# Block products for two more tiles of batch 0, and a new order of the work beside them

## The chip, the cores and the metric

The kernel runs on one core of a Trainium2 chip. The metric is the device time of one execution in microseconds (us). Before the change it is 262.92 us, the median of 3 runs (262.75 to 263.28).

## The reference, cut to what matters

Attention over blocks (4 batches, 8 heads, 768 rows, head size 64) is followed by a residual layer of 512 channels, in which one product mixes the 768 rows ("tokens") and two products the channels (512 to 2048 to 512). Keys and values are mixed block by block with an 8x8 matrix P, the result of five rounds of normalisation.

```
k_sorted = einsum('bhij,bhjcd->bhicd', P, k_b);  v_sorted likewise
scores = scale * q_b @ k_sb.T;  attn = softmax(scores);  x = attn @ v_sb
a1  = alpha1 * x + beta1
u   = x + lam * einsum('ts,bsd->btd', w_tok, a1)
a2  = alpha2 * u + beta2
out = u + lam * (relu(a2 @ w_ch1) @ w_ch2)
```

## The kernel before, in words

**Stages.** Every instruction of TensorE (PE), VectorE (DVE), ScalarE (ACT), GpSimd (POOL) and of the queue of SyncE (SP) is kept in the order in which the program issues it: the class Engine at line 55 records each one, which is why the profile gives one line, L65, for all, and groups are told apart by their tiles. The last loop of the program (lines 1055 to 1072) goes over 4 batches b and two halves hf of 384 rows each. A half has 16 units "h" (h_unit, line 763: four 128x384 matmuls from a2T and W1p into a buffer h_ps, and a ReLU on ACT into the halves hTa and hTb), and then the second channel product, phase "c".

**The second channel product.** In batch 0 it is done tile by tile (ch_unit, line 766): a tile of 128 rows takes 16 matmuls of 128x512, hT against W2p, and one VectorE addition. From batch 1 on it is done for two tiles at once (ch_pair, line 831): seven products of eight 128x256 matmuls instead of two times sixteen 128x512, named px, py, pz, px, pz, px, py after the buffers that they fill. They use sums and differences of the two tiles (block_sums, line 814: four VectorE operations for each part of the eight slices) and of the quarters of W2p (block_weights, line 798: eight operations of 128x1024 into TWa and TWb, once). Eight VectorE additions add_out take the products out, and some of the products must wait until an earlier addition has read their buffer. The pair numbers 0, 1 and 2 stand for tiles (1,2), (3,4) and (0,5).

**What is put beside it.** The attention of the next batch and the token product stand between the units. They are entered in a table by put(b, hf, kind, n, ...) (line 965): after unit n of phase "h", or after step n of phase "c", run() (line 968) issues the list of that slot. The slots are written out by hand in lines 974 to 1041. What matters here:

- mix_v and mix_k (lines 547, 562) make the mixed values and keys: a few matmuls into mix_ps or kmix_ps, and on ACT one cast for mix_v, four for mix_k into kT. bounce_v and back_v write the values to memory and read them back in another layout, on SP.
- score (line 419) fills sc_ps, and ACT takes the exponential. pv (line 479) multiplies by the values into x_ps; VectorE makes a reciprocal (rcb) and a product (x). After two of them, tails copies three blocks and first_affine does two operations (a): this is what flush and flush_one issue (line 509).
- moe_tok (line 715) is the token product, 6 matmuls of 128x512 into tok_ps, then u on VectorE and a 16-bit copy on ACT; moe_cross turns that copy round with three transposing DMAs on SP (uT), and moe_affine makes a2T of it for the next half.
- scale_weights (line 786) multiplies W2p by lam in four VectorE operations of 128x2048.

**Buffers.** PSUM has two pools: psA with 2 buffers (scores, x_ps, mix_ps, kmix_ps) and psB with 4 (h_ps, tok_ps, ch_ps, px, py, pz). An instruction that takes a buffer waits until its last reader is done.

Of the kernel before, what the change touches and what calls it, by code (L numbers as in the profile page):

```python
# [16 lines left out]
def kernel(  # L17
# [22 lines left out]
    B, H, S, D = q.shape  # L40
# [34 lines left out]
    act = Engine(nc.scalar)  # L75
# [11 lines left out]
    def psa(shape, dtype, name):  # L87
        return pools["psA"].tile(shape, dtype, name=name, tag="psA")
# [458 lines left out]
    def mix_v(b, n, eng):  # L547
        if n == 0:
            mixed[b] = att.tile([128, HB, D], F16, name="mixed", tag="qn" if b == B - 1 else "sums", bufs=1 if b == B - 1 else 2)
        ps = psa([128, 2, 512], FT, "mix_ps")  # L550
        raw = raw_of[(b, 1)][:].rearrange("p t d -> p (t d)")
        for m in range(2):
            pe.matmul(
                ps[:, m, :], bigM[b][:].rearrange("p a x -> p (a x)"),
                raw[:, n * 1024 + m * 512:n * 1024 + (m + 1) * 512], start=True, stop=True,
            )
        eng(
            mixed[b][:, n * 16:(n + 1) * 16, :].rearrange("p t d -> p (t d)"),
            ps[:].rearrange("p m f -> p (m f)"),
        )  # L560

    def mix_k(b, n, engs):
        if n == 0:
            kT_of[b] = att.tile([128, H4, NB, BLK], F16, name="kT", tag="kT", bufs=1)
        ps = psa([128, 8, 128], FT, "kmix_ps")
        raw = raw_of[(b, 0)]
        for tp in range(8):
            pe.matmul(
                ps[:, tp, :], raw[:, 16 * n + 2 * tp:16 * n + 2 * tp + 2, :].rearrange("p t d -> p (t d)"),
                bigP[b][:].rearrange("p a t g i -> p (a t g i)"), start=True, stop=True,  # L570
            )
        dst = kT_of[b][:].rearrange("p g i (th tp par) -> p th (g i) tp par", th=2, par=2)
        for par in range(2):
            for h2 in range(2):
                engs[2 * par + h2](
                    dst[h2 * 64:h2 * 64 + 64, :, :, 8 * n:8 * n + 8, par],
                    ps[par * 64:par * 64 + 64, :, h2 * 64:h2 * 64 + 64].rearrange(
                        "p n (th c) -> p th c n", th=2
                    ),
                )  # L580

    def bounce_v(b):
        for th in range(2):
            sp.dma_start(
                vscr[b, :, th * HB:(th + 1) * HB, :], mixed[b][th * 64:(th + 1) * 64, :, :],
            )
# [128 lines left out]
    def moe_tok(b, kt, ps):  # L715
        u32 = u_of[b]
        tok_part(b, kt, 0, C, ps)
        if b not in u16_of:
            u16_of[b] = moep.tile([128, NT, C], F16, name="u16", tag="u16", bufs=1)
        dve.scalar_tensor_tensor(  # L720
            u32[kt], tok_of[(b, kt)][:], 1.0 / GAIN, x_of[b][:, kt, :], op0=ALU.mult, op1=ALU.add,
        )
        act.copy(u16_of[b][:, kt, :], u32[kt])

    def moe_cross(b, hf):
        uT = uT_of[(b, hf)] = att.tile([128, CT, 384], F16, name="uT", tag="uT", bufs=2)
        for m in range(3):
            sp.dma_start_transpose(
                uT[:, :, m * 128:(m + 1) * 128], u16_of[b][:, 3 * hf + m, :],
            )  # L730

    def moe_affine(b, hf):
        for ci in range(CT):
            affine(b, hf, ci, uT_of[(b, hf)][:, ci, :], act if b and hf else dve)
# [3 lines left out]
    HK = HT // 2  # L738
# [24 lines left out]
    def h_unit(b, hf, m):  # L763
        h_part(b, hf, m, range(CT))
# [200 lines left out]
    def put(b, hf, kind, n, *todo):  # L965
        at.setdefault((b, hf, kind, n), []).extend(todo)
# [18 lines left out]
    pairs = [("s", 0), ("s", 2), ("p", 0), ("s", 4), ("p", 2), ("s", 6), ("p", 4), ("p", 6)]  # L985
    for b in range(1, B):
        p = b - 1
        if b == 1:
            for n in range(3):
                put(0, 0, "h", 11 + n, lambda n=n: mix_v(1, n, act.copy))  # L990
                put(0, 0, "c", 3 + 3 * n, lambda n=n: mix_k(1, n, (act.copy,) * 4))
            put(0, 0, "h", 13, lambda: bounce_v(1))
            put(0, 0, "c", 1, lambda: back_v(1))
            for g in range(H4):
                put(0, 0, "c", (4, 7, 10, 10)[g], lambda g=g: q_turn_late(1, g, (dve.tensor_copy, act.copy)[g % 2]))
            put(0, 0, "c", 11, lambda: loads(2))
            seq = [("s", 0), ("s", 1), ("s", 2), ("p", 0), ("s", 3), ("p", 1), ("p", 2), ("s", 4), ("p", 3), ("s", 5),
                   ("p", 4), ("s", 6), ("p", 5), ("s", 7), ("p", 6), ("p", 7)]
            for at_, (kind, n) in enumerate(seq):
                put(0, 1, "h", at_, (lambda n=n: score(1, n // 2, n % 2, psa)) if kind == "s" else (lambda n=n: pv(1, n // 2, n % 2)))  # L1000
        else:
            for n in range(3):
                put(p - 1, 1, "c", 1 + n, lambda b=b, n=n: mix_v(b, n, act.copy))
                put(p - 1, 1, "c", ((3, 6, 8), (4, 7, 10))[b - 2][n], lambda b=b, n=n: mix_k(b, n, (act.copy,) * 4))
            put(p - 1, 1, "c", 3, lambda b=b: bounce_v(b))
            put(p - 1, 1, "c", 7, lambda b=b: back_v(b))
            for kt in range(NT):
                put(*((0, 1, "h", 13) if b == 2 else (1, 0, "c", 1)), lambda b=b, kt=kt: q_cross(b, kt))
            if b + 1 < B:
                put(p, 0, "h", 3, lambda b=b: loads(b + 1))  # L1010
            for (kind, n), at_ in zip(
                pairs, ((0, "h", 0), (0, "h", 3), (0, "h", 5), (0, "h", 8), (0, "h", 11), (0, "c", 0), (0, "c", 2), (1, "h", 1)),
            ):
                for i in range(2):
                    f = (lambda b=b, n=n + i: score(b, n // 2, n % 2, psa)) if kind == "s" else (lambda b=b, n=n + i: pv(b, n // 2, n % 2))
                    put(p, *at_, f)
            for at_ in ((0, "h", 6), (0, "h", 7), (0, "h", 12), (0, "h", 13), (0, "c", 4), (0, "c", 5), (1, "h", 2), (1, "h", 3)):
                put(p, *at_, flush_one)
        if b == 1:
            put(p, 1, "h", 15, flush)  # L1020
        put(p, 1, "h", 3, lambda b=b: moe_start(b))
        for kt in range(3):
            put(p, 1, *(("c", 4) if b == 1 else ("h", 7 + 2 * kt)), lambda b=b, kt=kt: moe_tok(b, kt, psb))
        put(p, 1, *(("c", 4) if b == 1 else ("h", 11)), lambda b=b: moe_cross(b, 0))
        put(p, 1, "c", 8 if b == 1 else 6, lambda b=b: moe_affine(b, 0))
        for kt in range(3):
            put(b, 0, "h", 2 * kt, lambda b=b, kt=kt: moe_tok(b, 3 + kt, psb))
        put(b, 0, "h", 4, lambda b=b: moe_cross(b, 1))
        put(b, 0, "c", 2, lambda b=b: moe_affine(b, 1))

    for g, m in enumerate((12, 12, 13, 13)):
        put(0, 0, "h", m, lambda g=g: scale_weights(g))
    for n, at_ in enumerate(((0, 1, "c", 7),) * 4 + ((0, 1, "c", 9),) * 4):
        put(*at_, lambda n=n: block_weights(n))
    for b in range(1, B):
        for hf in range(2):
            for at_, lo, hi in ((8, 0, 4), (14, 4, 7), (15, 7, 8)):
                at.setdefault((b, hf, "h", at_), []).insert(0, lambda b=b, hf=hf, lo=lo, hi=hi: block_sums(b, hf, lo, hi))
        put(b, 1, "h", 11, lambda b=b: block_sums(b, 2, 0, 4))
        for at_, lo, hi in ((0, 4, 7), (5, 7, 8)):  # L1040
            put(b, 1, "c", at_, lambda b=b, lo=lo, hi=hi: block_sums(b, 2, lo, hi))

    for m in range(3):
# [10 lines left out]
    for b in range(B):  # L1054
        for hf in range(2):
            for i in range(HT):
                if b or hf or i > 2:
                    h_unit(b, hf, i // 2 + HK * (i % 2) if b else i)
                    run(b, hf, "h", i)
            slot = iter(range(14))  # L1060

            def step(b=b, hf=hf, slot=slot):
                run(b, hf, "c", next(slot))

            if b:
                for n in ((0,), (1, 2))[hf]:
                    ch_pair(b, n, step)
                continue
            for kk in range(3):
                for part in range(4):  # L1070
                    ch_unit(b, hf, kk, (4 * part, 4 * part + 4))
                    step()


# [28 lines left out]
```

## Time and profile before

| | us |
|---|---|
| median of 3 runs | 262.92 |
| the profiled execution | 262.59 |
| its span, from the first to the last instruction | 260.8 |
| TensorE busy, of the span | 248.4 |
| VectorE busy | 175.0 |
| ScalarE busy | 154.6 |
| granted TensorE clock, as a share of full speed | 0.997 |

The 1.8 us between the span and the time of that execution lie around the program. Matmuls are pipelined, so that the busy time of TensorE is not its work at full rate: of eight matmuls in a row the distance from start to start is what counts. In the timeline the bracket behind an instruction tells how long its engine was idle before it and what ended that. A wait in the list of waits is put down to what came last.

By stage, from the timeline of TensorE: 0 to 56 us the start and the first half of batch 0's units; 56 to 70 its second product; 70 to 86.5 the units of the second half, with batch 1's scores; 86.5 to 104 its second product, with the token product of batch 1; then batch 1 (104 to 160), batch 2 (160 to 213) and batch 3 (213 to 261).

### The profile page before, as it was taken

To read this page: it belongs to the slowest core of one execution; us is meant where nothing else is said; L and a number is where in the kernel's file an instruction comes from. 1 tells how busy PE (TensorE), PEld (TensorE's weight loads), DVE (VectorE), ACT (ScalarE), POOL (GpSimd) and SP (SyncE) were. 2 spreads that over 40 slices of the span, in tenths; PEclk is the share of its full clock that TensorE was granted. 3 is DMA by queue.
4 is the path that set the end of the run, shared out by engine and by line. 5 is a ranking of instruction groups with operands and counts; after the bars stand their busy time and mean duration, and the time that the engine had idled before them with its cause. 6 is when DMAs were issued, how large, how long until landed. Compare 5 with 4: busy or idle time off the path is not lost.

```text
span 260.8 us, 5951 instructions
## 1 busy us (share of the span) xinstructions
PE 248.4 (95%) x2371; PEld 159.8 (61%) x2371; DVE 175.0 (67%) x467; ACT 154.6 (59%) x282; POOL 44.3 (17%) x67
## 2 busy tenths in 40 slices
PE   8998899999999999999899999999899899999994
PEld 2566665555655544456665797568656775686783
DVE  6695889486438845759975964299966763462863
ACT  3567767565987588497464686888255004847400
POOL 8759303600091000074000000000000000000000
PEclk9999999999999999999999999999999999999998
DMA  6999999998999967979974169610202132111022
GB/s 101 211 204 187 208 206 215 203 139 186 172 176 176 121 143 171 152 132 182 136 118 119 20 146 169 133 23 0 80 18 45 42 96 69 23 40 40 3 80 80
DMA packets 67535, 31.07 MB, mean 119 GB/s; under 512 B 56674, under 2 KB 63218, under 8 KB 67508
## 3 DMA queue, kind: packets, MB, share of 16 engines
q0 software_dynamic: 26352, 15.34, 45.2%
q1 hardware_dynamic: 41060, 15.33, 33.8%
q8 instruction: 18, 0.29, 0.5%
q14 instruction: 9, 0.07, 0.1%
q10 hardware_dynamic: 96, 0.03, 0.1%
HBM read 32.79 MB, written 8.65 MB: 159 GB/s over the span
## 4 chain that ended last, share of the span: by engine, by line
PE 54%; DVE 19%; issue 2%; SPq 1%; DMA 1%; ACT 0%; DVEq 0%; ACTq 0%
PE h_ps L65 20%; PE tok_ps L65 9%; PE px L65 7%; DVE x L65 6%; PE py L65 5%; PE ch_ps L65 5%; DVE sums L65 4%; PE pz L65 4%; DVE a L65 2%; DVE ost L65 2%; DVE hTa L65 1%; PE kmix_ps L65 1%; PE x_ps L65 1%; PE sc_ps L65 1%; SPq L65 1%
## 5 line engine op out<-in xcount | busy, mean ns | idle before, releaser
L65 PE MATMUL h_ps<-a2T,W1p 128*128 128x384 bf16 x512 | 94.1, 326 | 0.6 <-DVE a2T L65 0.6
L65 PEld LDWEIGHTS <-W1p 128*128 128x128 bf16 x512 | 48.0, 98 | 32.7 <-issue 1.5
L65 ACT ACTIVATE hTa<-h_ps 128x384 f16<-128x384 f32 x64 | 31.3, 494 | 32.4 <-PE h_ps L65 31.5
L65 ACT ACTIVATE hTb<-h_ps 128x384 f16<-128x384 f32 x64 | 31.3, 491 | 6.7 <-PE h_ps L65 6.7
L65 DVE SCALAR_TENSOR_TENSOR u<-tok_ps,x 128x512 f32<-128x512 f32 x21 | 14.5, 691 | 29.7 <-PE tok_ps L65 29.7
L65 PE MATMUL tok_ps<-a,w_tokT 128*128 128x512 f16 x126 | 30.3, 379 | 0.0
L65 ACT CAST kT<-kmix_ps 64x512 f16<-64x512 f32 x36 | 25.7, 713 | 6.6 <-PE kmix_ps L65 6.2
L65 ACT ACTIVATE et<-sc_ps 96x768 f16<-96x768 f32 (+1 forms) x32 | 24.8, 807 | 3.2 <-PE sc_ps L65 3.2
L65 ACT CAST u<-u 128x512 f16<-128x512 f32 x21 | 13.0, 619 | 20.8 <-DVE u L65 20.8
L65 PEld LDWEIGHTS <-sums 128*128 128x128 f16 x216 | 21.0, 98 | 5.1 <-issue 1.7
L65 PEld LDWEIGHTS <-hTa 128*128 128x128 f16 x192 | 18.5, 98 | 8.9 <-issue 2.3
L65 PEld LDWEIGHTS <-hTb 128*128 128x128 f16 x200 | 18.6, 98 | 6.9 <-issue 0.8
L65 PEld LDWEIGHTS <-w_tokT 128*128 128x128 f16 x126 | 12.3, 98 | 13.1 <-issue 0.2
L65 DVE TENSOR_TENSOR x<-x_ps,rcb 96x512 f16<-96x512 f32 x24 | 16.5, 686 | 0.8
L65 POOL DMA_DIRECT2D qn<-in_q_dram x18 | 16.0, 910 | 4.0 <-DMA raw<-in_v_dram 3.9
L65 DVE TENSOR_TENSOR sums<-hTa,hTb 128x512 f16<-128x512 f16 (+2 forms) x27 | 8.9, 328 | 10.0 <-ACT hTb L65 10.0
L65 PEld LDWEIGHTS <-et 96*128 96x128 f16 (+4 forms) x288 | 11.9, 100 | 5.0 <-DVE x L65 2.2
L65 PE MATMUL x_ps<-Vs,et 96*128 96x65 f16 (+4 forms) x288 | 13.0, 195 | 1.6 <-DVE x L65 0.9
L65 PE MATMUL warm_ps<-wz 128*128 128x512 f16 x36 | 11.9, 466 | 1.2 <-DVE wz L65 1.2
L65 DVE SCALAR_TENSOR_TENSOR ost<-px,u 128x256 f32<-128x256 f32 x27 | 11.2, 416 | 1.9 <-PE px L65 1.9
L65 PE MATMUL ch_ps<-W2p,hTb 128*128 128x512 f16 x48 | 12.2, 379 | 0.2
L65 ACT CAST mixed<-mix_ps 128x1024 f16<-128x1024 f32 x9 | 9.1, 1013 | 4.9 <-PE mix_ps L65 4.8
(139 smaller groups left out, 351.2 us busy)
## 6 DMA issues: line engine op xcount, KB each, us to landing
out_dram<-ost SPq DMA_DIRECT2D x23, 192.0 KB, 2.5
raw<-in_v_dram POOLq DMA_DIRECT2D x6, 384.0 KB, 6.8
raw<-in_k_dram POOLq DMA_DIRECT2D x6, 384.0 KB, 10.2
qn<-in_q_dram POOLq DMA_DIRECT2D x18, 128.0 KB, 10.8
vscr<-mixed SPq DMA_DIRECT2D x6, 384.0 KB
Vs<-vscr SPq DMA_DIRECT2D x3, 768.0 KB
W1p<-in_moe_w_ch_dram POOLq DMA_DIRECT2D x4, 512.0 KB, 11.6
W2p<-in_moe_w_ch_dram POOLq DMA_DIRECT2D x4, 512.0 KB, 17.4
```

The lines of the kernel that those rows point to most:

```text
L65: ins = getattr(self.eng, name)(*args, **kwargs)
```

## The change

- In the second half of batch 0 tile 5 is still done by ch_unit; it comes first now. Tiles 3 and 4 are done by one ch_pair in place of two ch_units. Its block_sums stand in that half's units 8, 14 and 15, at the front of their slots, and the units there are issued alternately for hTa and hTb.
- block_weights moves from the second half of batch 0 (steps 7 and 9) to the first half (steps 5, 7, 9 and 11), two operations a step. scale_weights moves forward from units 12 and 13 to 10, 11 and 12.
- For batch 2, mixing the values and their way to memory moves one step forward (steps 0 to 2), and the first mix_k moves from step 3 to step 4. The token product of batch 1 goes from step 4 to step 3.
- For batches 2 and 3, the scores and pv of the batch before's first half move by a unit or a few steps: the third pair of scores from unit 8 to 7, the second pair of pv from 11 to 10, the third pv from step 2 to step 4, the last from unit 1 to unit 2 of the second half; the tails with them.
- Of pair 2's block_sums in batches 1 to 3 the second and third parts go from steps 0 and 5 to 4 and 6. moe_affine for batches 2 and 3 goes from step 6 to step 8.

```diff
-                put(p - 1, 1, "c", 1 + n, lambda b=b, n=n: mix_v(b, n, act.copy))
-                put(p - 1, 1, "c", ((3, 6, 8), (4, 7, 10))[b - 2][n], lambda b=b, n=n: mix_k(b, n, (act.copy,) * 4))
-            put(p - 1, 1, "c", 3, lambda b=b: bounce_v(b))
+                put(p - 1, 1, "c", b - 2 + n, lambda b=b, n=n: mix_v(b, n, act.copy))
+                put(p - 1, 1, "c", ((4, 6, 8), (4, 7, 10))[b - 2][n], lambda b=b, n=n: mix_k(b, n, (act.copy,) * 4))
+            put(p - 1, 1, "c", b, lambda b=b: bounce_v(b))
...
-                pairs, ((0, "h", 0), (0, "h", 3), (0, "h", 5), (0, "h", 8), (0, "h", 11), (0, "c", 0), (0, "c", 2), (1, "h", 1)),
+                pairs, ((0, "h", 0), (0, "h", 3), (0, "h", 5), (0, "h", 7), (0, "h", 10), (0, "c", 0), (0, "c", 4), (1, "h", 2)),
...
-            for at_ in ((0, "h", 6), (0, "h", 7), (0, "h", 12), (0, "h", 13), (0, "c", 4), (0, "c", 5), (1, "h", 2), (1, "h", 3)):
+            for at_ in ((0, "h", 6), (0, "h", 7), (0, "h", 11), (0, "h", 12), (1, "h", 0), (1, "h", 1), (1, "h", 3), (1, "h", 4)):
                 put(p, *at_, flush_one)
...
-            put(p, 1, *(("c", 4) if b == 1 else ("h", 7 + 2 * kt)), lambda b=b, kt=kt: moe_tok(b, kt, psb))
-        put(p, 1, *(("c", 4) if b == 1 else ("h", 11)), lambda b=b: moe_cross(b, 0))
-        put(p, 1, "c", 8 if b == 1 else 6, lambda b=b: moe_affine(b, 0))
+            put(p, 1, *(("c", 3) if b == 1 else ("h", 7 + 2 * kt)), lambda b=b, kt=kt: moe_tok(b, kt, psb))
+        put(p, 1, *(("c", 3) if b == 1 else ("h", 11)), lambda b=b: moe_cross(b, 0))
+        put(p, 1, "c", 8, lambda b=b: moe_affine(b, 0))
...
-    for g, m in enumerate((12, 12, 13, 13)):
+    for g, m in enumerate((10, 11, 12, 12)):
         put(0, 0, "h", m, lambda g=g: scale_weights(g))
-    for n, at_ in enumerate(((0, 1, "c", 7),) * 4 + ((0, 1, "c", 9),) * 4):
+    for n, at_ in enumerate(((0, 0, "c", 5),) * 2 + ((0, 0, "c", 7),) * 2 + ((0, 0, "c", 9),) * 2 + ((0, 0, "c", 11),) * 2):
         put(*at_, lambda n=n: block_weights(n))
-    for b in range(1, B):
-        for hf in range(2):
+    for b in range(B):
+        for hf in range(0 if b else 1, 2):
             for at_, lo, hi in ((8, 0, 4), (14, 4, 7), (15, 7, 8)):
                 at.setdefault((b, hf, "h", at_), []).insert(0, lambda b=b, hf=hf, lo=lo, hi=hi: block_sums(b, hf, lo, hi))
+        if b == 0:
+            continue
         put(b, 1, "h", 11, lambda b=b: block_sums(b, 2, 0, 4))
-        for at_, lo, hi in ((0, 4, 7), (5, 7, 8)):
+        for at_, lo, hi in ((4, 4, 7), (6, 7, 8)):
             put(b, 1, "c", at_, lambda b=b, lo=lo, hi=hi: block_sums(b, 2, lo, hi))
...
-                    h_unit(b, hf, i // 2 + HK * (i % 2) if b else i)
+                    h_unit(b, hf, i // 2 + HK * (i % 2) if b or hf else i)
...
-            for kk in range(3):
+            for kk in ((0, 1, 2), (2,))[hf]:
                 for part in range(4):
                     ch_unit(b, hf, kk, (4 * part, 4 * part + 4))
                     step()
+            if hf:
+                ch_pair(b, 1, step)
+                step()
```

## Prediction

> **What bounds the kernel now.** I read the chain of waits first, then the busy time by stage, then what TensorE waits for, then the timelines of TensorE (PE), VectorE (DVE) and ScalarE (ACT). The shares of the chain:
>
> ```profile
> PE 54%; DVE 19%; issue 2%; SPq 1%; DMA 1%; ACT 0%; DVEq 0%; ACTq 0%
> ```
>
> TensorE is the bound, but a fifth of the chain runs over VectorE. Where, the stages show (stretch, its length, then busy time and instructions of PE, weight loads, DVE, ACT, POOL):
>
> ```profile
> 70.30:86.50 16.20, 15.94 (x194) 9.08 (x193) 10.08 (x25) 13.37 (x26) 7.59 (x11) 1.00 1.35 181
> 86.50:104.10 17.60, 17.04 (x102) 8.27 (x99) 10.76 (x24) 13.24 (x19) 0.00 (x0) 1.00 0.97 143
> 104.10:130.40 26.30, 25.13 (x251) 16.29 (x251) 21.18 (x55) 17.33 (x32) 7.59 (x11) 1.00 1.55 151
> 130.40:160.20 29.80, 29.80 (x243) 21.51 (x241) 20.98 (x59) 20.25 (x34) 0.00 (x0) 1.00 0.57 112
> ```
>
> The stages from 70 to 130 each lose some time on TensorE, the one from 130 none. TensorE's waits name the places:
>
> ```profile
> PE px L65 <- DVE ost L65: 2.1, 3, 1.0
> ...
> PE pz L65 <- DVE ost L65: 1.1, 2, 0.7
> ...
> PE x_ps L65 <- DVE x L65: 0.9, 2, 0.4
> ...
> PE h_ps L65 <- DVE a2T L65: 0.6, 1, 0.6
> ```
>
> Most are products that wait for an addition on VectorE to read their buffer; the change's moves aim there. The clock is 1.00 in these stages, so it plays no part.
>
> **The change part by part.** Times are those of the old profile ("old clock"), and I follow by how much the new kernel is late (+) or early (-).
>
> *scale_weights earlier.* Two rows of the timeline, PE and DVE:
>
> ```profile
> 58.22 2.16 PE L65 MATMUL ch_ps<-W2p,hTb 128*128 128x512 f16 x8
> ```
> ```profile
> 54.67 4.63 DVE L65 TENSOR_TENSOR W2p<-W2p,lam 128x2048 f16<-128x2048 f16 x4
> ```
>
> Eight such matmuls take 1.89 in the row before, here 2.16, and start 0.27 late: 0.54 lost to waiting for W2p, whose last quarter ends at 59.3. In the new order VectorE does, from 51.00: u 0.61, lam 0.45, W2p 1.14, u 0.61, W2p 1.14, u 0.61, W2p 2 x 1.14: the end is 57.84. The last quarter is wanted at 56.23 + 12 x 0.216 = 58.82. So **-0.54** (none, if the quarters come late again).
>
> *block_weights.* Eight operations at 0.60 from start to start (100.28 to 101.48 for two) are 4.8 us more in the stage from 57 to 70, where VectorE is busy 8.3 of 13.3. Worked through in order, with the waits for qt_ps and ch_ps, the last ends at 71.8; what is queued behind is the first rcb of the second half, at 73.9. So 0, hidden by idle VectorE; without that cover 0.6 for each operation too many. The stage that they leave gains nothing: VectorE sat idle 2.7 us there at 113.
>
> *Two ch_units become one ch_pair.* 32 matmuls of 512 at 0.216 (eight in 1.73 in the chain at 86.65) are 6.91; 56 of 256 at 0.109 (px at 145.19, py at 146.07: 0.873 for eight) are 6.11: **-0.81**.
>
> The Trainium skill, "TensorE: Matmul & The Clock Gate", section Back-to-back issue gap, speaks against this: it gives pairs of weight load and matmul a sustained spacing of about 81 ns at 128 columns and 131 ns at 512, so that narrow products hardly save. By an estimate between those two (98 ns at 256) the exchange would be 32 x 131 against 56 x 98 ns, a loss of 1.3 us. The rows say 216 and 109 ns, and I go by them.
>
> *The sums in the second half of batch 0.* Their price is not in this stage yet, but the same operations are in batch 1: 1.59 (118.04 to 119.63), 1.32 (to 124.53) and 0.79 (to 125.32), together 3.70. VectorE works here from 74.5 to 91.35 with few gaps; two of 0.53 (before 81.59 and 85.78, where it waits for x_ps) are filled, the one of 1.08 before 76.48 lies ahead of the sums. So the last `a` ends at 91.35 - 0.54 + 3.70 - 1.06 = 93.45. Bounds: nothing filled, 94.5; all of it beside TensorE's waits, 92.4. I take 93.45, from the gaps of the very stage.
>
> Before, the 18 tok_ps matmuls started at 92.55 and did not wait:
>
> ```profile
> 92.55 4.05 PE L65 MATMUL tok_ps<-a,w_tokT 128*128 128x512 f16 x18
> ```
>
> Now they stand one step earlier and wait for `a`: they run from 93.5 to 97.4. On the way TensorE waits at x_ps and mix_ps, but all of that lies inside this sum. Behind tok come seven products, 6.11, and three kmix of 0.445: the half ends at 104.85.
>
> *The wait for a2T goes.*
>
> ```profile
> 104.10 1.19 PE L65 MATMUL h_ps<-a2T,W1p 128*128 128x384 bf16 x4 [0.56 <-DVE a2T L65]
> ```
>
> These four took 1.19 where others take 0.81; they followed a2T at its pace, so that the old stage really ended at 104.49. The chain gives 6.9 from the last tok matmul (96.61) to the landing of uT (103.54); at that pace it lands now at 104.3, and SP's queue holds it up less, since the values' way to memory is issued two steps sooner. a2T stands on VectorE in front of three additions, which end near 106; the units that take those buffers come at 106.8. So batch 1 begins at 104.85, **+0.36**.
>
> *What is late next: kT.* All three mix_k now stand behind tok:
>
> ```profile
> 98.81 5.81 ACT L65 CAST kT<-kmix_ps 64x512 f16<-64x512 f32 x8 [0.83 <-PE kmix_ps L65]
> ```
>
> Twelve casts at 0.726 are 8.7. ACT is free for them when the third copy of u is done, 1.38 after tok (97.99 - 96.61): 98.8 + 8.7 = 107.5. The scores want kT at 104.85 + 0.65 + 1.30 = 106.8 and began at 106.58 before. Late: **+0.97**. Two small waits at the next scores (0.12 and 0.19, near 111) should go, since the exponentials are then done sooner in relation: +0.66 at the first x_ps (bounds 0 and +1.3).
>
> *The new order in the first halves of batches 1 and 2.* Here the old waits were largest; the second row is the token product of the half that follows:
>
> ```profile
> 125.79 1.03 PE L65 MATMUL px<-TWa,sums 128*128 128x256 f16 x8 [0.19 <-DVE ost L65]
> ...
> 128.65 1.03 PE L65 MATMUL px<-TWb,hTa 128*128 128x256 f16 x8 [0.95 <-DVE ost L65]
> ...
> 136.11 1.46 PE L65 MATMUL tok_ps<-a,w_tokT 128*128 128x512 f16 x6
> ```
> ```profile
> 135.26 0.56 DVE L65 TENSOR_TENSOR a<-a,betaB 128x768 f16<-128x768 f16 x1
> ```
>
> VectorE works without a break from 114.05 to 135.82, and tok at 136.1 needs that last `a`. Moving x_ps behind the fifth product lets the sixth start 0.6 earlier, but the second px still waits for px's addition behind the sums (125.32), and VectorE now idles 0.36 and 0.53 while it waits for px and pz. Worked through: additions to 128.08, two x to 129.76, three additions, copies and two `a` to 132.55, two x to 134.34, copies and `a` to 136.14. tok starts at 136.2, after waiting some 0.7: **+0.1**, the wait has only moved. For batch 2 the same: 191.18 against 191.05, **+0.13**. One difference in batch 1: its first three copies took 1.10 (115.84) beside POOL's q loads, and 0.72 in batch 2. The mixed values are read back some 2.5 us sooner, so these loads should lie ahead of the copies: **-0.41** (bounds -0.41 and 0).
>
> *Pair 2's sums later, a2T later.* In batches 2 and 3 the fifth product waits for pz's addition behind the sums (0.86 and 0.57 more than its pace, at 203.6 and 247.6). With the sums behind that addition both waits go. In batch 2 a2T (1.15) now stands between the second pair's py and pz additions: 210.52 where pz wants it at 209.74, so 0.8 comes back; **-0.1**. Batch 3 has no a2T: **-0.57**. In batch 1 kmix between the products covers it: 0.
>
> **The sum:** 0.66 - 0.41 + 0.1 + 0.13 - 0.1 - 0.57 = -0.19. The profiled execution took 262.59 (span 260.8), so 262.4; its run lay 0.33 below the median, and on the median's scale I predict **262.7**.
>
> **The rivals.** (1) *Slower: VectorE's queue ahead of tok.* Every us by which the last `a` ends after 93.45 goes to tok, kT and the end one to one. If the sums fill no gap, 1.06 is added: 263.8. For: the queue is nearly full, and four flushes stand in it; POOL loads beside it, and copies were seen at 1.10. Against: the gaps are seen in this very stage. It decides from 0.7 on. (2) *Faster: the order really pays in batches 1 and 2.* If VectorE gets through its queue 0.7 sooner in each (shorter steps between dependent additions, no idling for px and pz), tok doesn't wait: -1.4, 261.3. Against: its work there is the same. (3) *Faster: kT is not late,* because ACT gets to its casts earlier than 98.8: -0.7, 262.0. (4) *The change doesn't do what it says:* the block product gains nothing here, as its products wait for additions: +0.8, 263.5.
>
> **How the numbers follow.** Forecast 0.40, rival 1 0.25, rival 2 0.18, rival 3 0.08, rival 4 0.09. A measurement of this kernel can tell about 0.2%, 0.53 us, from no change, so "same" is 262.4 to 263.45: the forecast case, 0.40; faster 0.26 (2 and 3), slower 0.34 (1 and 4). The range takes in all rivals and a bound of 0.4 (the copies) on top of the slowest: 261.3 to 264.2.
>
> **What would show it.** In the new profile: no wait for W2p near 58; VectorE unbroken from 79 to 93 and tok waiting for `a` at 93.5; no wait for a2T at the start of batch 1, but one for kT at the first scores; tok of batches 2 and 3 waiting for `a`, in place of the third px product's wait; pz in batch 3 without a wait. I am wrong if tok of batch 1 starts before 92.9 or after 94.2, or if the waits at px go without coming back at tok.

## The result, and the profile after

The changed kernel takes **264.34 us**, the median of 7 runs (263.84 to 265.85); beside it the kernel before takes 262.92 (7 runs, 262.39 to 264.00). The ratio is 1.0047, with a 95% interval of 1.0025 to 1.0070: slower by 0.7 to 1.8 us, and 0.14 above the top of the range on record. The profiled execution took 264.52 (span 262.7), against 262.59 (260.8) before: 1.9 later. The time outside the span is no longer 1.8 us in every run: in the seven kernels with the block product in batch 0 (this one, e1, e5, e6, e10, e11, e13) some runs have 2.0 to 2.9 us of it, on the mean 1.9 to 2.2, where all runs of the others have 1.7 to 1.9. No view shows what lies there; the cause stays open.

The chain of waits, the line of shares by engine:

```profile
PE 64%; DVE 25%; ACT 6%; issue 3%; DVEq 0%
```

The shares are not alike as they stand: the chain before is followed back to 57 us alone (its shares add up to 77%), this one to the start. From 57 us on, the pieces of VectorE in the chain add up to 48.6 us before and 61.8 now. The stages, cut at the same events as before (stretch, length, then busy time of PE, weight loads, DVE, ACT, POOL):

```profile
70.14:87.70 17.56, 16.02 (x193) 9.26 (x192) 13.54 (x33) 13.51 (x26) 7.69 (x11) 1.00 1.43 189
87.70:105.45 17.75, 16.70 (x126) 10.63 (x122) 12.34 (x34) 11.13 (x16) 0.00 (x0) 1.00 0.93 145
105.45:131.28 25.83, 24.77 (x253) 16.32 (x250) 16.95 (x45) 19.77 (x35) 7.59 (x11) 1.00 1.48 158
131.28:161.99 30.71, 29.83 (x242) 21.34 (x240) 22.12 (x64) 20.16 (x34) 0.00 (x0) 1.00 0.51 99
```

The first stage is the one that the sums entered: VectorE's work rose from 10.08 to 13.54 and the stage from 16.20 to 17.56, while TensorE does the same. The last one was free of waits before and now loses 0.88. TensorE's waits:

```profile
PE tok_ps L65 <- DVE a L65: 2.2, 3, 0.9
PE x_ps L65 <- DVE x L65: 1.4, 3, 0.5
...
PE pz L65 <- DVE ost L65: 0.9, 1, 0.9
PE sc_ps L65 <- DVE x L65: 0.7, 1, 0.7
PE px L65 <- DVE ost L65: 0.7, 2, 0.5
PE sc_ps L65 <- ACT kT L65: 0.5, 1, 0.5
```

px fell from 2.1 to 0.7 and the wait for a2T is gone, but tok, which waited nowhere, waits 2.2 in three places. The timeline of TensorE, the places in order:

```profile
94.12 4.05 PE L65 MATMUL tok_ps<-a,w_tokT 128*128 128x512 f16 x18 [0.45 <-DVE a L65]
...
108.30 0.51 PE L65 MATMUL sc_ps<-qT,kT 64*128 64x96 f16 x15 [0.52 <-ACT kT L65]
...
127.27 1.03 PE L65 MATMUL px<-TWa,sums 128*128 128x256 f16 x8 [0.51 <-DVE ost L65]
...
138.04 1.47 PE L65 MATMUL tok_ps<-a,w_tokT 128*128 128x512 f16 x6 [0.88 <-DVE a L65]
...
193.44 1.47 PE L65 MATMUL tok_ps<-a,w_tokT 128*128 128x512 f16 x6 [0.88 <-DVE a L65]
...
213.23 1.03 PE L65 MATMUL pz<-W2p,sums 128*128 128x256 f16 x8 [0.92 <-DVE ost L65]
```

Every mechanism on record is there: tok behind the last `a`, kT late, the wait at px come back at tok, a2T in front of the addition that pz waits for. The sizes are another matter. The table follows TensorE from event to event in the two traces (after minus before, the lateness that each section adds):

| section | forecast | trace |
|---|---|---|
| start to the first ch_ps (56.23 before) | 0 | +0.39 |
| W2p, to the second half of batch 0 | -0.54 | -0.53 |
| its h units and products, to tok | +1.49 | +1.71 |
| tok to the start of batch 1 (a2T's pace counted) | -0.59 | -0.61 |
| to the first x_ps of batch 1 (kT) | +0.30 | +0.59 |
| to tok of batch 2 (order, copies) | -0.31 | +0.38 |
| to tok of batch 3 (order) | +0.13 | +0.46 |
| to batch 3 (sums and a2T) | -0.10 | +0.11 |
| batch 3 | -0.57 | -0.56 |
| sum | -0.19 | +1.94 |

### The profile page after: what moved, and what is told of

Its sections match the earlier page's. It is cut to its first block, busy times and chain, and to the rows that moved or that the text cites. A ratio compares the mean times of both kernels' runs of the same rounds, so it can differ in the third digit from the quotient of the medians.

```text
span 262.7 us, 6021 instructions
## 1 busy us (share of the span) xinstructions
PE 247.4 (94%) x2395; PEld 162.1 (62%) x2395; DVE 181.5 (69%) x485; ACT 155.3 (59%) x282; POOL 44.3 (17%) x67
## 4 chain that ended last, share of the span: by engine, by line
PE 64%; DVE 25%; ACT 6%; issue 3%; DVEq 0%
PE h_ps L65 19%; PE tok_ps L65 11%; DVE x L65 10%; PE px L65 7%; PE pz L65 5%; DVE a L65 5%; PE py L65 4%; PE warm_ps L65 4%; PE ch_ps L65 4%; DVE sums L65 4%; ACT kT L65 3%; DVE ost L65 2%; PE x_ps L65 2%; PE sc_ps L65 2%; DVE rcb L65 1%
## 5 line engine op out<-in xcount | busy, mean ns | idle before, releaser
L65 PEld LDWEIGHTS <-sums 128*128 128x128 f16 x240 | 23.4, 98 | 5.4 <-issue 2.1
L65 DVE TENSOR_TENSOR sums<-hTa,hTb 128x512 f16<-128x512 f16 (+2 forms) x30 | 9.9, 329 | 10.0 <-ACT hTb L65 10.0
L65 DVE SCALAR_TENSOR_TENSOR ost<-px,u 128x256 f32<-128x256 f32 x30 | 12.5, 418 | 4.1 <-PE px L65 4.1
L65 PE MATMUL sc_ps<-qT,kT 64*128 64x96 f16 (+1 forms) x256 | 10.0, 205 | 1.5 <-DVE x L65 0.7
```

Of the source, the lines that this page charges most:

```text
L65: ins = getattr(self.eng, name)(*args, **kwargs)
```

## The experiments

Each ratio is to the kernel before on the same chip; in us it is worked out as (ratio - 1) x 263. The first four take the change apart.

**e1, batch 0 alone.** The edits of scale_weights, block_weights, block_sums of batch 0, ch_pair, tok and the slots of mix_v, mix_k and bounce_v; lines 1011 to 1018, the later parts of pair 2's sums and moe_affine as before.

> The change's edits in batch 0 alone: W2p scaled earlier, block weights earlier, block product with its sums in the second half, tok one step earlier, keys and values of batch 2 moved with it. Batches 1 and 2 keep their old order, and pair 2's sums and a2T their old places. Theory A (the lateness is made in batch 0, by 3.7 us of sums on VectorE ahead of the last a; what the profile of the changed kernel shows up to the first x_ps of batch 1, +1.55, less the 0.39 that it was already late at the start): about +1.2 on the kernel before, 264.1, and tok of batch 1 waits for a. Theory B (my working on record holds for this part, and the loss lies in the later batches): +0.66 at the first x_ps and -0.41 at the copies, 262.9 to 263.5.

Measured: 263.88, ratio 1.0030 (1.0006 to 1.0055), +0.8. In its trace tok of batch 1 waits 0.45 for `a`, and 1.43 is added between the first ch_ps and the first x_ps of batch 1; 0.63 of that are slower copies that also come without the change (the last section), so 0.80 is left, between B's 0.66 and A's 1.2. The mechanism of A is there, but its size is nearer to B's: of the changed kernel's own 1.16 (1.55 less 0.39), 0.36 are slower copies too, which leaves 0.80 there as well, against the 0.66 on record. (The profiled execution, 265.37, lies 1.5 above e1's median. Behind that first x_ps it lost another 0.89 up to the next tok, some 0.7 of it at an a2T that came late from ScalarE, which stands in no other kernel's waits.)

**e2, the slots alone.**

```diff
-                pairs, ((0, "h", 0), (0, "h", 3), (0, "h", 5), (0, "h", 8), (0, "h", 11), (0, "c", 0), (0, "c", 2), (1, "h", 1)),
+                pairs, ((0, "h", 0), (0, "h", 3), (0, "h", 5), (0, "h", 7), (0, "h", 10), (0, "c", 0), (0, "c", 4), (1, "h", 2)),
-            for at_ in ((0, "h", 6), (0, "h", 7), (0, "h", 12), (0, "h", 13), (0, "c", 4), (0, "c", 5), (1, "h", 2), (1, "h", 3)):
+            for at_ in ((0, "h", 6), (0, "h", 7), (0, "h", 11), (0, "h", 12), (1, "h", 0), (1, "h", 1), (1, "h", 3), (1, "h", 4)):
```

> Only the new places of score pairs, x_ps products and flushes in the first halves of batches 1 and 2; all else as before. Theory A (these moves cost by themselves, since VectorE idles for px and pz in front of two x additions that it used to do there: 0.38 and 0.46 in the two traces): about +0.8, 263.7, with tok of batches 2 and 3 waiting for a. Theory B (they cost only because the kernel was already late in batch 0; alone the wait just moves): +0.2, 263.1. Theory C (the order pays): -1.4, 261.5.

Measured: 263.59, ratio 1.0028 (1.0011 to 1.0045), +0.7. From the first x_ps to the next tok it takes 23.01 (22.52 before) and 22.57 (22.11): +0.49 and +0.46. The first copies took 1.12 here and 1.10 before, so that the order alone costs 0.47 and 0.46. Theory A; B and C fall. The third px does not wait any more, tok does, as in this line of its trace:

```profile
137.10 1.25 PE L65 MATMUL tok_ps<-a,w_tokT 128*128 128x512 f16 x5 [0.88 <-DVE a L65]
```

**e3, pair 2 alone.**

```diff
-        put(p, 1, "c", 8 if b == 1 else 6, lambda b=b: moe_affine(b, 0))
+        put(p, 1, "c", 8, lambda b=b: moe_affine(b, 0))
-        for at_, lo, hi in ((0, 4, 7), (5, 7, 8)):
+        for at_, lo, hi in ((4, 4, 7), (6, 7, 8)):
```

> Only pair 2's later sums, and a2T of batches 2 and 3 at the eighth step. Theory A (parts add up, as on record): batch 3's wait at pz goes, 0.57, and batch 2's comes back as a wait behind a2T, -0.1: -0.7, 262.2. Theory B (batch 2 loses more behind a2T than its old wait, as the changed kernel's 0.9 to 1.1 at 213 us suggests): -0.4 or less, 262.5.

Measured: 262.42, ratio 0.9979 (0.9963 to 0.9994), -0.55. Batch 3 gains 0.57, batch 2 loses 0.11 by a wait of 0.93 behind a2T. The time lies between the theories, the trace with B. The parts add up to 1.0 (0.8 + 0.7 - 0.55) against 1.2 for the whole.

**e4, two gains without a2T's move.** W2p scaled earlier, pair 2's sums later, a2T at its old step 6.

```diff
-    for g, m in enumerate((12, 12, 13, 13)):
+    for g, m in enumerate((10, 11, 12, 12)):
-        for at_, lo, hi in ((0, 4, 7), (5, 7, 8)):
+        for at_, lo, hi in ((4, 4, 7), (6, 7, 8)):
```

> The kernel before with W2p scaled earlier and pair 2's sums later, but a2T at its old sixth step, ahead of those sums, and nothing else. Theory A (each of these takes a wait away for good): 0.54 near 58 us, 0.86 in batch 2, 0.57 in batch 3: -1.9, 261.0, and no wait at pz in either batch. Theory B (a wait taken away early only makes the next one longer, as it did with the order of batches 1 and 2): -0.6 or less, 262.3 or more.

Measured: 262.57, ratio 0.9992 (0.9975 to 1.0009): no gain that shows. The 0.54 of W2p arrives at 70 us and is more than gone when batch 1 has begun: 0.39 went to slower copies (the last section), and 0.34 to a2T, which begins only 0.45 sooner than before on the profile's clock (103.22 against 103.67), on which this run was 0.63 ahead from the start. In batch 2 the wait moved to pair 2's second px, whose buffer is read behind a2T and the last sums:

```profile
209.66 1.03 PE L65 MATMUL px<-TWa,sums 128*128 128x256 f16 x8 [0.70 <-DVE ost L65]
```

**e7, a2T of batch 3 on ScalarE.** On top of e4:

```diff
-            affine(b, hf, ci, uT_of[(b, hf)][:, ci, :], act if b and hf else dve)
+            affine(b, hf, ci, uT_of[(b, hf)][:, ci, :], act if b and (hf or b == B - 1) else dve)
```

> The kernel e4 (W2p scaled earlier, pair 2's sums later) with batch 3's a2T (1.15 on VectorE) made by ScalarE, which is idle from 201 to 214 us. Theory A (in batch 2 the sums and a2T together are too long for the gaps between the additions: e4 waits 0.93 behind them at px, the changed kernel 1.09 at pz): the wait goes without coming back, -0.75 against e4, 261.8. Theory B (the third place, or a2T arriving later from ScalarE, takes it over): no gain against e4, 262.5.

Measured: 261.51, ratio 0.9931 (0.9905 to 0.9957), -1.8: below both kernels, with an interval clear of 1. Theory A. ScalarE's timeline shows that the longer operation there costs nothing:

```profile
201.67 2.50 ACT L65 ACTIVATE a2T<-uT,ab2col 128x384 bf16<-128x384 f16 x4 [0.71 <-DMA uT<-u]
213.29 0.49 ACT L65 ACTIVATE hTa<-h_ps 128x384 f16<-128x384 f32 x1 [9.12 <-PE h_ps L65]
```

TensorE goes through all fourteen products without a wait, and the section from tok to batch 3 takes 21.31 instead of 22.29. So the loss behind a2T was VectorE's queue, and nothing later took the gain back. In batch 1, where a2T stays on VectorE ahead of the last sums, the same product still comes 0.21 late (155.10 to 156.18).

**e5, the sums of batch 0 behind the last `a`.** On the changed kernel:

```diff
-            for at_, lo, hi in ((8, 0, 4), (14, 4, 7), (15, 7, 8)):
-                at.setdefault((b, hf, "h", at_), []).insert(0, lambda b=b, hf=hf, lo=lo, hi=hi: block_sums(b, hf, lo, hi))
+            for at_, lo, hi in ((("h", 8), 0, 4), (("h", 14) if b else ("c", 3), 4, 7), (("h", 15) if b else ("c", 3), 7, 8)):
+                at.setdefault((b, hf, *at_), []).insert(0, lambda b=b, hf=hf, lo=lo, hi=hi: block_sums(b, hf, lo, hi))
```

> The changed kernel with the last two groups of sums of batch 0 (1.32 and 0.79 us) put behind the last a on VectorE's queue, next to the token product, where VectorE idles (0.94, 0.60 and 0.60 at 95 to 98 us). Theory A (these sums stand ahead of the last a, and every us of them goes to tok one to one): the waits at mix (0.37) and tok (0.45) go, those up to 87 us stay: -0.8, 263.5. Theory B (the lateness of batch 0 comes from the sums at the eighth unit and from copies beside POOL's loads): -0.2 or less, 264.1.

Measured: 264.82, ratio 1.0066 (1.0033 to 1.0098). The waits at mix and tok went as theory A has it: from the first ch_ps product to tok it takes 5.15, where the changed kernel takes 6.42. But the time did not fall. The next wait appeared at the start of batch 1:

```profile
105.63 1.19 PE L65 MATMUL h_ps<-a2T,W1p 128*128 128x384 bf16 x4 [1.60 <-DVE a2T L65]
```

SP's queue shows why (start, time that SP spent issuing, number of DMAs):

```profile
85.00 8.66 SPq L65 DMA_TRANSPOSE qT<-qn  x6
93.75 1.18 SPq L65 DMA_DIRECT2D vscr<-mixed  x2
95.03 3.07 SPq L65 DMA_DIRECT2D out_dram<-ost  x2
98.19 3.82 SPq L65 DMA_TRANSPOSE uT<-u  x3
```

The queue is full from 85 to 102. ScalarE had the three copies of u done between 96.8 and 98.0, but their transposes stand behind q's and the stores. In the changed kernel they begin at 98.22, the same moment; there VectorE was late enough to hide it. (Right after this wait the granted clock of this execution fell: it was 0.50 to 0.58 from 106.6 to 109.6 and 0.84 on the mean from 105.6 to 116.5. The comparison above ends before. Five of e5's twelve runs have a mean clock of 0.986 to 0.994 and took 265.6 to 267.0; the seven at 0.997 or more took 263.4 to 264.9, their median 263.96. So part of the 264.82 is the clock.)

**e10, the stores behind the transposes of u.** On top of e5:

```diff
-        act_out(out[b, kt * 96:(kt + 1) * 96, :], ost[0:96, :])
-        act_out(out[b, TAIL + kt * 32:TAIL + (kt + 1) * 32, :], ost[96:128, :])
+        def put_out():
+            act_out(out[b, kt * 96:(kt + 1) * 96, :], ost[0:96, :])
+            act_out(out[b, TAIL + kt * 32:TAIL + (kt + 1) * 32, :], ost[96:128, :])
+        if hf:
+            put(0, 1, "c", 4, put_out)
+        else:
+            put_out()
```

> The kernel e5 (changed kernel, sums behind a) with the two stores of the third 512-column product issued behind the transposes of u on SP's queue instead of ahead of them. Theory A (in e5 and in the changed kernel SP could issue the transposes of u only at 98.2, behind the transposes of q until 93.7, the values' way out and these stores of 3.07 us, while u was ready at 96.8): the transposes begin 1.4 or more earlier, the wait for a2T at the start of batch 1 (1.60 in e5) goes, 263.2. Theory B (the landing, not the queue, is late): the wait stays, 264.8.

Measured: 264.39, ratio 1.0032 (1.0003 to 1.0061), +0.8; 0.9 less than e5. In its trace the transposes begin 1.35 sooner and batch 1 starts at 103.90 without a wait:

```profile
93.98 1.18 SPq L65 DMA_DIRECT2D vscr<-mixed  x2
96.84 3.99 SPq L65 DMA_TRANSPOSE uT<-u  x3
100.92 1.00 SPq L65 DMA_DIRECT2D out_dram<-ost  x2
```

Theory A for the mechanism, but not for the time: the 263.2 was not reached, and what it gained against the changed kernel (0.4) is inside the intervals. Nor are the 0.9 against e5 the stores alone, since e5's clock is in them. Part of e10's time lies outside the span: the median span is 0.25 above that of the kernel before beside it (261.85 and 261.6), the time 0.84.

**e11, the block product mended, on top of e7.** The edits of batch 0 from e1 with those of e5 and e10.

> The kernel e7 with the block product in batch 0, its sums behind the last a and the stores behind the transposes of u; the order of batches 1 and 2 is the old one. It tells whether the block product pays once its sums no longer stand ahead of tok. Theory A: 32 products of 512 against 56 of 256 save 0.81, of which the waits for x (about 0.7 to 0.8 at 83 and 86 us) and for kT (0.5) take more back: 0 to +0.6 against e7, 261.5 to 262.1. Theory B: the 0.81 arrive: 260.7.

Measured: 261.79, ratio 0.9955 (0.9933 to 0.9978), -1.2, against -1.8 for e7: no gain, the intervals overlap. The block product does save its 0.81 (from tok's end its seven products and three kmix take 7.45, as worked out), but the sums that it needs bring back waits for x at 84 and 87 us and for kT at 108: from the start of the second half of batch 0 to the first x_ps of batch 1, less the slower copies, it takes 0.05 more than e7. Theory A.

**e6 and e8, the copies x<-x on ScalarE.** e6 on the changed kernel, e8 on e7:

```diff
-            dve.tensor_copy(x[96:128, a:a + 4:3, c], x[32 * a:32 * a + 32, 6:8, c])
+            (act.copy if x is not x_of.get(0) else dve.tensor_copy)(x[96:128, a:a + 4:3, c], x[32 * a:32 * a + 32, 6:8, c])
```

> The changed kernel with the copies x<-x of batches 1 to 3 (0.72 for three, four times a batch) on ScalarE instead of VectorE. Theory A (volume: VectorE has more to do from the first x_ps to tok than TensorE, 21.8 us without a break, whatever the order): the waits at px (0.51, 0.18) and at tok (0.88, 0.88) go, -2.4, 261.9. Theory B (order: the last a comes late because its last x_ps comes late, and a trip over ScalarE makes it no earlier): 264.0 to 264.8, with tok still waiting for a.

> The kernel e7 with the copies x<-x of batches 1 to 3 on ScalarE too; the order of batches 1 and 2 is that of the kernel before. Theory A (VectorE's volume, not the order, made the old waits at px, 0.19, 0.95 and 0.95): they go, -2.1 against e7, 259.7. Theory B (order): no gain against e7, 261.8 or more.

Measured: 269.93, ratio 1.0235 (1.0192 to 1.0278), and 264.92, ratio 1.0068 (1.0039 to 1.0096). Neither theory had this. The three copies take 1.23 on ScalarE, and VectorE stands at the `a` behind them; two lines of VectorE's timeline in e6:

```profile
118.61 0.56 DVE L65 TENSOR_TENSOR a<-x,alphaB 128x768 f16<-128x768 f16 x1 [1.35 <-ACT x L65]
...
124.32 0.56 DVE L65 TENSOR_TENSOR a<-x,alphaB 128x768 f16<-128x768 f16 x1 [1.29 <-ACT x L65]
```

This says nothing yet about volume against order, so the copies were given time:

**e9 and e12, the copies on ScalarE in time.** On e7; three of four copy groups of batches 2 and 3, and new flush slots. The first of the two new lists is e9's, the second e12's; they differ in one number:

```diff
-            late.append(lambda: tails(x_of[b], c))
+            late.append(lambda: tails(x_of[b], c, act.copy if b > 1 and g < 3 else dve.tensor_copy))
-            for at_ in ((0, "h", 6), (0, "h", 7), (0, "h", 12), (0, "h", 13), (0, "c", 4), (0, "c", 5), (1, "h", 2), (1, "h", 3)):
+            for at_ in ((0, "h", 9), (0, "h", 11), (0, "c", 0), (0, "c", 2), (0, "c", 5), (1, "h", 0), (1, "h", 2), (1, "h", 3)):
+            for at_ in ((0, "h", 9), (0, "h", 11), (0, "c", 0), (0, "c", 4), (0, "c", 5), (1, "h", 0), (1, "h", 2), (1, "h", 3)):
```

> The kernel e7 with three of the four copy groups x<-x of batches 2 and 3 on ScalarE, each issued some units after its x, and the a behind them again later, so that neither engine stands waiting for the other (e6 and e8 had VectorE wait 1.3 to 1.4 for each). Theory A (VectorE's volume from the first x_ps to tok, 21.8 us, makes the waits at px): 3 x 0.72 leave VectorE, the waits 0.19, 0.95 and 0.95 at px go and tok waits for nothing: -2.1 against e7, 259.4. Theory B (the order and the lateness of each x_ps make them): no gain against e7 or a wait at tok, 261.5 or more.

> The kernel e9 with the second a of each first half (two operations, 1.06) two steps later on VectorE's queue: behind the additions of px and pz, not between the two x and px's addition, where e9 still waited 1.31 for px. Theory A (what stands ahead of px's addition makes the wait at px; with 1.06 less there it is 0.3 or less, and the copies that left VectorE leave room ahead of tok): -0.9 per batch against e9, two batches, 260.0. Theory B (volume alone decides, the a only moves to the queue ahead of tok and tok waits for it): no gain against e9, 261.8.

Measured: e9 took 261.80, ratio 0.9958 (0.9928 to 0.9988), -1.1, no better than e7's -1.8 (0.62 later by the traces, 0.27 of it already ahead of the first ch_ps) although 2.16 of work left VectorE in each batch; e12 260.17, ratio 0.9879 (0.9843 to 0.9915), **-3.2**. TensorE's timeline at the third px product in e9:

```profile
128.79 1.03 PE L65 MATMUL px<-TWb,hTa 128*128 128x256 f16 x8 [1.31 <-DVE ost L65]
```

The same product in e12:

```profile
128.18 1.03 PE L65 MATMUL px<-TWb,hTa 128*128 128x256 f16 x8 [0.25 <-DVE ost L65]
```

The number in brackets is the wait. Two operations of `a` between x and px's addition in e9 made the wait longer than in the kernel before (0.95); behind the additions they cost nothing, tok doesn't wait, and the section from x_ps to tok takes 21.39 (22.52 before), the one in batch 2 21.40 (22.11). Room on VectorE without the order gave nothing (e9), the change's order without room cost 0.7 (e2); this one took both, room and the addition that TensorE waits for ahead of the rest of the queue. Its order with the copies left on VectorE was not run, so that the order's own part is not shown.

**e13, the changed kernel with the old slots in batches 1 and 2.** The edit of e2, undone.

> The changed kernel with the old places of score pairs, x_ps products and flushes in batches 1 and 2; all its other edits stay. Theory A (these places cost 0.38 and 0.46 in its trace, as they did alone in e2): -0.8 against the changed kernel, 263.5, with px waiting 0.95 in both batches and tok for nothing. Theory B (they help once batch 0 is late): 264.3 or more.

Measured: 263.69, ratio 1.0018 (0.9996 to 1.0040), +0.5 against the changed kernel's +1.2. In its trace the sections from x_ps to tok take 22.39 and 22.12, px waits 0.95 and tok for nothing. Theory A for the waits. By the ratios the order is 0.7 to 0.8 of the loss, with intervals that overlap; by the traces it is 0.44 and 0.45 in the two batches, once the copies (0.96 here, 1.03 in the changed kernel) are taken out.

## Why the forecast was wrong, step by step

**The step that failed: "The new order in the first halves of batches 1 and 2".** It was put at +0.1 and +0.13 for the order and -0.41 for the copies, -0.18 together; it measured 0.38 + 0.46 = +0.84: the order cost 0.45 and 0.46, the copies gave 0.07. e2 shows the order alone (0.47 and 0.46), e13 shows it taken back. That is 1.0 of the 2.1 by which the two traces miss the forecast. That the wait moves from px to tok was right; two sizes were not:

- The walk through VectorE's queue was 0.36 short. It holds to 0.01 until the two x are done (131.23 here; by the walk 129.76, plus the 1.55 by which batch 1 is late, less 0.07 by faster copies: 131.24). Then three additions and the copies' start were put 0.33 to 0.34 apart, 1.0 in all, and took 1.30: an addition that reads what the one before it wrote starts 0.51 after it, and the copies 0.46 after an addition. Both spacings stood in the profile of before (125.32 to 125.84; 128.70 to 129.16) and were not used. The other 0.06 are at the end: the last copies and two `a`, put at 1.80, took 1.87 (136.11 to 137.98). The queue came out 0.61 longer than before, and tok's slack of 0.29 (from 135.82 to 136.11) shrank to 0.06: 0.38. VectorE's timeline before:

```profile
125.32 0.42 DVE L65 SCALAR_TENSOR_TENSOR ost<-px,u 128x256 f32<-128x256 f32 x1
125.84 0.42 DVE L65 SCALAR_TENSOR_TENSOR ost<-py,ost 128x256 f32<-128x256 f32 x1
...
128.70 0.42 DVE L65 SCALAR_TENSOR_TENSOR ost<-pz,ost 128x256 f32<-128x256 f32 x1
129.16 0.69 DVE L65 COPY x<-x 32x256 f16<-32x256 f16 x3
```

And after:

```profile
131.23 0.41 DVE L65 SCALAR_TENSOR_TENSOR ost<-px,ost 128x256 f32<-128x256 f32 x1
131.56 0.41 DVE L65 SCALAR_TENSOR_TENSOR ost<-px,u 128x256 f32<-128x256 f32 x1
132.07 0.42 DVE L65 SCALAR_TENSOR_TENSOR ost<-py,ost 128x256 f32<-128x256 f32 x1
132.53 0.69 DVE L65 COPY x<-x 32x256 f16<-32x256 f16 x3
...
137.42 0.56 DVE L65 TENSOR_TENSOR a<-a,betaB 128x768 f16<-128x768 f16 x1
```

- The first copies were to fall from 1.10 to 0.72, as POOL's q loads would lie ahead of them. The loads did begin 1.6 sooner, but the fifth of them waits for a DMA; it is issued from 117.06 to 117.94, and the copies, at 117.40, took 1.03.

None of the four rivals is what happened: the place of rival 1 lost 0.22 of the 2.1. Nor did the signs of being wrong come up, since tok of batch 1 began at 94.12, inside 92.9 to 94.2, and the wait at px did come back at tok.

**VectorE's queue ahead of tok.** The last `a` was to end at 93.45 on the old clock. It ended at 94.07 (93.51 and 0.56), less the late start of 0.39 at 93.68: 0.23 late, with copies at 78 us that took 0.36 more than in the profile of before. tok began at 93.73 on that clock, 0.23 after its forecast too. e5 confirms that the sums are what delays it.

**kT.** (The +0.97 is a slip of 0.05: 107.5 less 106.58 is 0.92.) Forecast late by 0.97 - 0.36 = 0.61 at the scores, measured 0.76; of the 0.31 that the next two waits were to give back, 0.17 came. The casts end at 108.24, where the forecast (107.5) plus tok's further lateness (0.62) has 108.1: the mechanism and the rate were right.

**The start of batch 1.** Right in time (-0.61 for -0.59), wrong in one reason: "SP's queue holds it up less". It holds it up more, since q's transposes and the stores stand in front until 98.2; VectorE hid that. e5 took the cover off and e10 the cause.

**Right:** W2p (-0.53 here and in e1, -0.54 in e4, for -0.54); block_weights at 0 (the last operation ended at 72.2, and VectorE idled until 74.4); the exchange of 32 wide for 56 narrow matmuls at -0.81; batch 3 (-0.56 for -0.57). The spacings of the Trainium skill, "TensorE: Matmul & The Clock Gate", section Back-to-back issue gap (about 131 ns at 512 columns, 81 ns at 128), by which narrow products hardly save, are not borne out: the products of eight matmuls of 256 begin 0.87 or 0.88 after one another in the changed kernel (98.00 to 105.45 with three kmix between), as before.

**Batch 2's sums and a2T** came out at +0.11 for -0.10: the addition lay 1.09 late, not 0.8. e7 removes it.

**The base was a lucky one.** 0.39 of the trace's difference lies ahead of the change; what grew there is a wait of one x_ps of the start that is put down to issue (0.39 before, 0.94 here; between 0.38 and 0.94 in the other runs), and its cause stays open. The copies at 78 us took 0.69 in the profile of before and 1.02 to 1.61 in every other profile in which VectorE makes them there. By the medians the change costs 1.2 to 1.4, not 1.9; that still leaves 1.4 to 1.6 of error, of which the step on the order and the copies is 1.0. Some 0.2 of the loss lie outside the span (1.97 on the mean of the seven runs), where the forecast had kept the 1.8.

## What to carry to other kernels

A walk through a full queue must use the spacing of dependent operations where they depend, since a wait that "only moves" costs whatever the walk is short by. Before reordering a stage, add up the busy time of the engine that is waited for: here VectorE worked 21.8 us without a break in a section of 22.5 us, and the new order alone did not pay (e2). Work that left VectorE did (a2T, and copies, to ScalarE), the copies when the result that TensorE waits for also came ahead in the queue (e12, not e9). When a cover is taken away, look into the DMA-issuing queue too: it was full for 17 us beside a TensorE that seemed to wait for VectorE alone.

## What the runs showed of the hardware

**POOL's DMA issues hold VectorE's copies, and the stage takes it one to one.** The three copies at 78 us in the profile of before, where POOL stood idle from 78.36 to 79.38, on VectorE's timeline:

```profile
78.35 0.69 DVE L65 COPY x<-x 32x256 f16<-32x256 f16 x3
```

POOL's timeline of the same execution:

```profile
77.48 0.88 POOL L65 DMA_DIRECT2D qn<-in_q_dram  x1 [0.47 <-DMA raw<-in_v_dram]
79.38 0.87 POOL L65 DMA_DIRECT2D qn<-in_q_dram  x1 [1.02 <-DMA raw<-in_v_dram]
```

The same three copies in e3, one by one, take 1.50 together:

```profile
78.28 0.63 DVE L65 COPY x<-x 32x256 f16<-32x256 f16 x1
78.92 0.22 DVE L65 COPY x<-x 32x256 f16<-32x256 f16 x1
79.15 0.63 DVE L65 COPY x<-x 32x256 f16<-32x256 f16 x1
```

POOL's timeline in e3, where five issues follow one another until 79.73, and the last two of them one by one:

```profile
75.27 4.46 POOL L65 DMA_DIRECT2D qn<-in_q_dram  x5
```
```profile
77.92 0.94 POOL L65 DMA_DIRECT2D qn<-in_q_dram  x1
78.78 0.95 POOL L65 DMA_DIRECT2D qn<-in_q_dram  x1
```

The first copy ends 0.05 after the end of one issue, the third 0.05 after the end of the next; the second, which began 0.14 after the start of an issue, took its usual 0.22. All traces agree: from 60 us on, 34 copies on VectorE took 0.37 to 0.74 instead of 0.22, and each began 0.23 to 0.59 after the start of a load issue of POOL and ended 0.02 to 0.06 after its end. Twenty that began 0.06 to 0.23 after such a start took 0.22. So what a copy loses is the rest of the issue, and how much a stage loses depends on where in the issues the copies fall.

Nothing in this stage differs between the two kernels. In the runs that keep it as it was, the copies took 0.39 (e4), 0.59 (e2), 0.72 (e12), 0.73 (e9), 0.80 (e7) and 0.81 (e3) more than before, and the stage was 0.39, 0.60, 0.74, 0.74, 0.80 and 0.81 longer. Sums, x and `a` kept their durations beside the same loads, and so did the copies on ScalarE in e6 (1.23 at 77.18 us, where POOL issues until 78.68, and 1.23 away from its loads at 133). The Trainium skill, "SBUF — State Buffer", section SBUF: two separate sides, says that VectorE in its two-port modes and GpSimd share one pair of ports, which one instruction holds to its end. These runs agree that the copies are held to the end of an issue; no view names the ports, and copies that began in an issue's first 0.2 us were not held.

**One operation, two engines.** a2T took 2.50 for four on ScalarE and 1.24 on VectorE, the three copies 1.23 and 0.69. The slower engine was the better place for a2T, since it had nothing else to do for 12 us.

**SP's issue time is a cost of its own.** Six transposes held the queue for 8.66, two stores for 0.99 (before) to 3.07 (e5); the same two stores, issued after the transposes of u, took 1.00 (e10).
